# Zero matmuls in a fused attention and feed-forward kernel: only into PSUM banks without a planned reader, and a larger part of each planned PE gap

## The chip, the core and the metric

The kernel runs on one core of one Trainium2 chip. The metric is the device time of one execution in microseconds (us). A profile shows one execution, instruction by instruction; its "span" is the time from the first to the last instruction, in us from its own start. Engines: PE does matmuls (and PEld its weight loads), DVE, ACT and POOL do elementwise work, SP issues transfers. PSUM is the memory that PE writes into.

## What is computed

Inputs: q, k and v (8 batches, 12 heads, 448 positions, 64 dimensions), two gains of 64, `w_in` (768 x 2048) and `w_out` (2048 x 768), all float32.

```python
q_n, k_n = rmsnorm(q, g_q), rmsnorm(k, g_k)          # over the 64 dimensions
scores = 1/8 * q_n @ k_n.T                           # per batch and head
attn = exp(scores - max); attn = attn / (sum(attn) + 1e-9)
x = (attn @ v), heads side by side                   # 3584 x 768
h = x @ w_in
out = (h * clip(h + 3, 0, 6) / 6) @ w_out            # 3584 x 768
```

## The kernel before

**The work.** The unit of attention is a pair of heads: 48 pairs P, six to a batch. For a pair, SP loads k, q (L509, L537, L503) and v (L516, L503). Squares `sq` (L558, L560), row sums `ssq` (L577, DVE) and the root `rs` (L583, L584, ACT) give the scale, and `qks` (L593, L600, L609) is the scaled q or k. For the first twelve pairs PE turns it by 64 x 64 transposes (L653) into a tile M, from which copies make `kq`, `kp` and `kb` (L522, L524, L525); later pairs are turned by a transfer. PE makes scores in S from `kp` or `kb` (L801, L806); ACT takes their exponential, `e` or `er` (L834); PE multiplies it with v and a column of ones, `va` or `var`, into X (L772, L890); DVE divides by the row sum (`rd` L908, `xn` L909, `xr` L913). `xn` is turned, for the first two batches by PE (L930), into `xT`. Then the feed-forward part: `w_in` against `xT` into M (L969), ACT's `t` (L975) and DVE's `gT` (L977), then `w_out` against `gT` (L994) and the copy `y`, which is stored.

**PSUM.** There are two score tiles S0 and S1 (of two banks each), one tile X of two banks, and two tiles M. The real results leave columns free: X's second bank holds results in its first 260 columns, S's first bank in its first 448. A wait is set by tile: any write into X waits for the earlier readers of X, whatever the columns.

**The order.** A planner lists every step with an estimate of its duration, goes over the list forward and backward, and fixes a start and an end for each step on each engine (`Plan.order`). The kernel is then written out in the order of the planned starts, so each engine's queue is in that order. By the plan the last step ends at 433.06 us. At run time only semaphores count, not the planned times.

**The zero matmuls.** `zero` is a tile of zeros. Where the plan leaves PE idle for more than 0.3 us before a planned start of 115 us (`FILL_TO`), `fill` (L1105 on) writes matmuls of `zero` with `zero` (L1112) into the free columns of X (240 wide), S0 or S1 (64 wide); they add zero to what stands there and change no result. `reads` holds, for each of the three places, the planned start and end of every step on another engine than PE that uses its tile. `fill` walks through the gap in planned time: it takes the first place of X, S0, S1 that it may use at that moment, and moves on by an estimate of what the matmul takes; if there is none, it moves on by 0.1 us:

```python
if not any(x - 0.05 < t0 < y + 0.2 for x, y in l):
    n = t.shape[-1]
    nc.tensor.matmul(out=t, lhsT=zero[:, 0:128], rhs=zero[:, 0:n], start=False, stop=False,
                     skip_group_check=True)
    t0 += n / 1200 if t0 < COLD else n / 2400 / FILL
```

So a place is refused only while one of its readers is running by the plan. A zero matmul written just after a reader's planned end waits for that reader by semaphore, and the next real matmul of PE's queue stands behind it.

Of the kernel before, what the change touches and what calls it, by code (L numbers as in the profile page):

```python
# [304 lines left out]
def kernel(  # L305
# [80 lines left out]
    plan = Plan(NUDGES, ENGINES, HOLD)  # L386
    add = plan.add

    FILL, FILL_FROM, FILL_TO, COLD = 0.7, 1.2, 115.0, 6.0
    XPE, TQ, MOVE = 2, 0.26, 12  # L390
    GATE, W_IN_AT, W_OUT_AT, W_STEP = 4, 6.0, 40.0, 4.3
    START, FIRST, PAIR = 9.0, 3.7, 2.1
# [709 lines left out]
    reads = [(t, [(s.start, s.end) for used in ring.log[k::ring.n] for s in used if s.eng != "PE"])  # L1102
             for ring, k, t in idle]

    def fill(t0, t1):  # L1105


        while t1 - t0 > 0.1:
            for t, l in reads:
                if not any(x - 0.05 < t0 < y + 0.2 for x, y in l):  # L1110
                    n = t.shape[-1]
                    nc.tensor.matmul(out=t, lhsT=zero[:, 0:128], rhs=zero[:, 0:n], start=False, stop=False,  # L1112
                                     skip_group_check=True)
                    t0 += n / 1200 if t0 < COLD else n / 2400 / FILL
                    break
            else:
                t0 += 0.1

    with tc.manual_schedule():
        nc.vector.memset(zero[:], 0.0)  # L1120
        for t in (X_r.bufs[0][:], S_r.bufs[0][:], S_r.bufs[1][:]):
            nc.vector.memset(t, 0.0)
        holder, free = None, FILL_FROM
        for s in order:
            if s.eng == "PE":
                if s.start < FILL_TO and s.start - free > 0.3:
                    fill(free, s.start - 0.1)
                free = s.end
            ins = s.fn(s.eng)
            if ins is not None and s.lock and s.eng in ("DVE", "POOL"):  # L1130
                if s.eng == "POOL" and holder is not None:
                    tc.add_manual_dep(ins.ins, holder.ins.name, mybir.DependencyInfo(
                        mybir.DependencyClass.Sync, mybir.DependencyReason.DATA), reason="port")
                holder = ins if s.eng == "DVE" else None
# [30 lines left out]
```

## Time and profile before

| | |
|---|---|
| median of five runs | 435.73 us (433.9 to 439.19) |
| profiled execution: its time, its span | 435.73 us, 433.8 us |
| mean granted PE clock | 0.996 |
| busy: PE, DVE, ACT, POOL | 96%, 56%, 58%, 48% |
| zero matmuls (L1112) | 98 into X, 50 into S |
| first matmul of the feed-forward part (L969) | at 48.36 us |
| last matmul ends | at 429.2 us |

The views used: the page's shares; the busy time by stretch, whose columns are the stretch and its length, busy us and instructions of PE, PEld, DVE, ACT and POOL, the granted PE clock (PEclk, 1.00 is full speed), the mean busy share of the core's 16 DMA engines (it passes 1 where packets overlap) and GB/s; the chain of waits, that is the work that ended last, followed back from step to step (start, length, engine, tile and line); the view of one line, with what PE stood idle for before it (total us, times); and the timeline (start, length, engine, line, operation, number of instructions, and in brackets an idle time ahead and what ended it). An entry of several matmuls is as long as from the first start to the last end, and their ends are modelled, so it overlaps its neighbour by up to 0.2 us.

### The profile page before, as it was taken

What the parts mean: (1) busy time and instruction counts of PE and PEld (TensorE: products, weight loads), DVE (VectorE), ACT (ScalarE), POOL (GpSimd) and SP (SyncE); (2) the same over time, 40 slices, a digit from 0 to 9 for tenths busy, and PEclk for the clock granted to TensorE, in tenths of its full rate; (3) what the DMA queues carried; (4) which work ended last, traced back from release to release, by engine and by line L of the source; (5) the groups of instructions that cost most, each with busy time, mean ns of one, the idle gap of its engine ahead of it and who ended that gap; (6) DMA issues with size and microseconds to landing.
All of it is one profiled execution on the core that took longest, in us unless ns stands there. A gap on an engine that the chain in (4) does not pass through costs nothing.

```text
span 433.8 us, 10149 instructions
## 1 busy us (share of the span) xinstructions
PE 416.3 (96%) x4057; PEld 244.1 (56%) x4057; DVE 241.4 (56%) x472; ACT 249.8 (58%) x454; POOL 210.1 (48%) x270
## 2 busy tenths in 40 slices
PE   7867999999999999999999999999999999999995
PEld 5545665655456665655556566655555565644563
DVE  6757786655685565637753676445754545344300
ACT  5948877657874776517663676427763656023211
POOL 5845576475957254757554663665856210000000
PEclk9989999999999999999999999999999999999999
DMA  8999999669777946796667787485474330310122
GB/s 223 230 233 271 245 237 204 165 138 222 180 182 127 206 111 154 170 221 149 139 154 210 139 151 184 109 213 141 100 172 106 77 73 19 82 52 0 38 73 73
DMA packets 114838, 64.75 MB, mean 149 GB/s; under 512 B 71272, under 2 KB 111336, under 8 KB 114792
## 3 DMA queue, kind: packets, MB, share of 16 engines
q1 hardware_dynamic: 107488, 57.83, 56.8%
q0 software_dynamic: 7296, 6.29, 9.0%
q8 instruction: 31, 0.51, 0.5%
q14 instruction: 15, 0.12, 0.1%
q10 hardware_dynamic: 8, 0.00, 0.0%
HBM read 45.61 MB, written 11.01 MB: 131 GB/s over the span
## 4 chain that ended last, share of the span: by engine, by line
PE 87%; DMA 5%; DVE 4%; SPq 1%; ACT 1%; issue 1%; POOL 0%; DVEq 0%; ACTq 0%; POOLq 0%
PE M L969 28%; PE M L994 28%; PE X L890 9%; PE S L801 7%; PE S L994 4%; PE S L969 2%; DMA vf<-in_v_dram 2%; PE X L994 2%; PE S L806 2%; PE X L772 1%; DMA kf<-in_k_dram 1%; PE X L969 1%; DMA qf<-in_q_dram 1%; PE M L653 1%; DVE ssq L577 1%; DVE xn L909 1%
## 5 line engine op out<-in xcount | busy, mean ns | idle before, releaser
L969 PE MATMUL M<-xT,w_in_sb 128*128 128x384 bf16 (+1 forms) x696 | 142.7, 350 | 0.2
L834 ACT ACTIVATE e<-S 128x896 bf16<-128x896 f32 x144 | 124.8, 914 | 30.3 <-PE S L801 30.0
L994 PE MATMUL M<-w_out_sb,gT 128*128 128x384 bf16 x736 | 129.5, 326 | 0.0
L994 PEld LDWEIGHTS <-gT 128*128 128x128 bf16 x896 | 84.7, 98 | 54.5 <-issue 0.7
L969 PEld LDWEIGHTS <-w_in_sb 128*128 128x128 bf16 x768 | 71.8, 98 | 63.9 <-issue 2.1
L975 ACT ACTIVATE t<-M 128x384 f32<-128x384 f32 (+1 forms) x116 | 62.5, 539 | 71.0 <-PE M L969 70.1
L977 DVE SCALAR_TENSOR_TENSOR gT<-t,M 128x384 bf16<-128x384 f32 (+1 forms) x116 | 71.0, 613 | 57.5 <-ACT t L975 56.0
L577 DVE TENSOR_REDUCE ssq<-sq 128x14 f32<-128x896 f32 (+1 forms) x49 | 51.7, 1061 | 5.9 <-POOL sq L560 4.5
L890 PE MATMUL X<-va,e 128*128 128x65 bf16 x1152 | 50.8, 194 | 3.9 <-POOL va L524 3.5
L890 PEld LDWEIGHTS <-e 128*128 128x128 bf16 x1152 | 44.7, 98 | 16.9 <-issue 8.3
L560 POOL TENSOR_TENSOR sq<-qf 112x512 f32<-112x512 f32 (+1 forms) x38 | 39.2, 1034 | 22.5 <-DVE kp L675 8.2
L524 DVE COPY y<-M 128x384 f32<-128x384 f32 x40 | 22.3, 558 | 42.6 <-PE M L994 41.8
L600 POOL TENSOR_TENSOR qks<-kf,rs 128x384 bf16<-128x384 f32 x36 | 29.8, 828 | 29.4 <-ACT rs L584 24.5
L560 POOL TENSOR_TENSOR sq<-kf 128x384 f32<-128x384 f32 (+1 forms) x40 | 33.4, 837 | 19.4 <-DVE kp L675 8.1
L801 PE MATMUL S<-kq,kp 64*128 64x448 bf16 x288 | 41.3, 357 | 0.5 <-ACT kq L522 0.3
L609 POOL TENSOR_TENSOR qks<-qf,rs 112x512 bf16<-112x512 f32 x36 | 37.6, 1045 | 7.3 <-ACT rs L584 5.6
L524 POOL CAST va<-vf 128x384 bf16<-128x384 f32 x46 | 23.1, 506 | 32.2 <-PE X L890 15.3
L909 DVE TENSOR_TENSOR xn<-X,rd 128x384 bf16<-128x384 f32 x48 | 26.8, 558 | 1.7
L834 ACT ACTIVATE er<-S 128x896 bf16<-128x896 f32 (+1 forms) x27 | 22.5, 833 | 8.3 <-PE S L806 8.2
L583 ACT ACTIVATE rs<-ssq 128x14 f32<-128x14 f32 (+1 forms) x49 | 10.5, 214 | 25.6 <-DVE ssq L577 25.3
L908 DVE RECIPROCAL rd<-X 128x8 f32<-128x8 f32 x48 | 9.9, 205 | 21.8 <-PE X L890 20.9
L1112 PE MATMUL X<-zero 128*128 128x240 bf16 x98 | 16.0, 302 | 5.9 <-DVE xn L909 2.5
(79 smaller groups left out, 302.1 us busy)
## 6 DMA issues: line engine op xcount, KB each, us to landing
qf<-in_q_dram SPq DMA_DIRECT2D x48, 224.0 KB, 3.8
kf<-in_k_dram SPq DMA_DIRECT2D x36, 192.0 KB, 3.5
vf<-in_v_dram SPq DMA_DIRECT2D x36, 192.0 KB, 3.3
out_dram<-y SPq DMA_DIRECT2D x18, 192.0 KB, 3.0
w_in_sb<-in_moe_w_in_dram POOLq DMA_DIRECT2D x4, 768.0 KB, 14.2
w_out_sb<-in_moe_w_out_dram POOLq DMA_DIRECT2D x4, 768.0 KB, 19.6
kf<-in_k_dram SPq DMA_DIRECT2D x12, 224.0 KB, 5.3
vf<-in_v_dram SPq DMA_DIRECT2D x24, 96.0 KB, 9.0
```

The source lines that it names most:

```text
L524: return (nc.vector if e == "DVE" else nc.gpsimd).tensor_copy(out=out, in_=x)
L560: return engines[e].tensor_tensor(out=o, in0=x, in1=x, op=MULT)
L577: lambda i0=i0, i1=i1, rows=rows: nc.vector.tensor_reduce(out=ssq[0:rows, i0:i1], in_=sq[0:rows, i0:i1], axis=AX_X, op=ADD),
L609: return engines[e].tensor_tensor(out=qks[0:PT, NS:QB].rearrange("p t (h d) -> p h t d", h=2), in0=qf[0:PT].rearrange("p (h t) d -> p h t ...
L801: fns.append(lambda ps=ps, a=a, t=t, kp=kp, rhs=rhs: nc.tensor.matmul(out=ps[:, a, 0:S], lhsT=kp[a * 64:a * 64 + 64, t * 128:(t + 1) * 128 ...
L834: lambda dst=dst, ps=ps, w=2 if whole else 1: nc.scalar.activation(out=dst, in_=ps[:, 0:w, 0:S], func=EXP), s, *(AVW[P] if t < NS else AVR ...
L890: nc.tensor.matmul(out=X[:, a, s * E1:(s + 1) * E1], lhsT=e[:, t, a, c0:c0 + 128], rhs=va[:, a * NS + t, :], start=False, stop=(t == NS - ...
L909: nc.vector.tensor_tensor(out=xn[:], in0=xv[:, 0:NS, :, 0:D], in1=rd[:, 0:NS].unsqueeze(3).to_broadcast([128, NS, 2, D]), op=MULT)
L969: nc.tensor.matmul(out=m[:, 0:n], lhsT=w_in_sb[:, kt, f * 128:(f + 1) * 128], rhs=X[:, kt, :], start=(kt == 0), stop=(kt == NKT - 1))
L975: r = add("ACT", 0.17 + n / 1200, due + span, lambda: nc.scalar.activation(out=t[:, 0:n], in_=m[:, 0:n], func=RELU, bias=0.5, scale=1.0 / ...
L977: g = add("DVE", 0.155 + n / 960, due + span, lambda: nc.vector.scalar_tensor_tensor(out=G[:, f, :], in0=t[:, 0:n], scalar=1.0, in1=m[:, 0 ...
L994: nc.tensor.matmul(out=m[:, 0:HALF], lhsT=G[:, f, i * 128:(i + 1) * 128], rhs=w_out_sb[:, f, cols], start=(f == 0), stop=(f == NFT - 1))
```

## The change

It touches `fill`, the call of it and two constants. A place may now be used only if each of its planned readers either starts after the next real PE step (`now`) or has ended at least 0.4 us before the moment in question. The share of a gap that is charged to a zero matmul (`FILL`) goes from 0.7 to 0.9, so more of them go into a gap; the moment until which PE's clock is taken as half (`COLD`) goes from 6.0 to 7.0 us; and gaps from 0.2 us on are filled.

```diff
-    FILL, FILL_FROM, FILL_TO, COLD = 0.7, 1.2, 115.0, 6.0
+    FILL, FILL_FROM, FILL_TO, COLD = 0.9, 1.2, 115.0, 7.0
...
-    def fill(t0, t1):
+    def fill(t0, t1, now):
...
-                if not any(x - 0.05 < t0 < y + 0.2 for x, y in l):
+                if all(x > now or y + 0.4 < t0 for x, y in l):
...
-                if s.start < FILL_TO and s.start - free > 0.3:
-                    fill(free, s.start - 0.1)
+                if s.start < FILL_TO and s.start - free > 0.2:
+                    fill(free, s.start - 0.1, s.start)
```

The plan itself does not change: the queues of DVE, ACT, POOL and SP hold the same instructions in the same order, and PE's real matmuls keep theirs. The zero matmuls of the built kernels differ in these gaps (by the step that follows the gap, with its start in the profile before):

| next real PE step | zero matmuls before | after |
|---|---|---|
| the gaps before 22 us, in all | 74 X | 82 X |
| L801 at 22.93 | 11 S1 | none |
| L772 at 31.15 | none | 1 S1 |
| L801 at 34.05 | 7 S1 | none |
| L801 at 39.37 | 5 X, 6 S1 | none |
| L653 at 43.87 | 2 X, 2 S1, 2 S0 | none |
| L930 at 47.59 | 2 X, 18 S1 | 33 S1 |
| L806 at 47.98 | 1 X, 4 S0 | 10 S0 |
| L969 at 50.74 | 4 X | 5 X |
| L969 at 59.22 | 2 X | 3 X |
| L806 at 64.45 | 3 X | 14 S1 |
| L969 at 55.15, L653 at 70.86 | none | 1 X each |
| L969 at 67.13 | none | 4 S0 |
| L801 at 73.98 | none | 3 S0 |

## The prediction

> **What bounds the kernel now.** I first read the page's busy shares (PE 96%, DVE, ACT and POOL 48 to 58%), then the busy time by stretch.
>
> ```profile
> 23.90:27.50 3.60, 0.09 (x6) 0.10 (x1) 0.69 (x2) 2.23 (x4) 0.95 (x2) 1.00 1.18 247
> 27.50:31.00 3.50, 3.49 (x59) 2.45 (x58) 1.63 (x5) 1.73 (x4) 2.83 (x5) 0.56 1.19 234
> 37.00:48.00 11.00, 7.69 (x184) 6.20 (x183) 8.24 (x19) 8.77 (x19) 6.53 (x9) 1.00 1.19 260
> 100.00:433.80 333.80, 328.74 (x2856) 186.54 (x2853) 175.09 (x331) 178.34 (x312) 145.39 (x173) 1.00 0.56 129
> ```
>
> The first number after the length is PE's busy time; PEclk comes before the DMA share. From 100 us on PE is idle only in the tail after the last matmul (429 us): whatever brings the dense stretch forward brings the end forward. The holes are before 48 us. The chain of waits says what stands in them:
>
> ```profile
> 17.35 9.03 DMA vf<-in_v_dram
> 27.51 1.20 PE X L890 x24
> ...
> 37.98 0.57 DVE xn L909
> 38.59 0.67 PE X L1112 x5
> ...
> 46.87 0.36 PE X L1112 x2
> 47.23 0.53 PE S L1112 x18
> 47.76 0.17 PE M L930 x3
> ```
>
> Until 27.5 us a load of V sets the pace. Behind it the zero matmuls (L1112) themselves stand on the chain, after the DVE operation that read their bank. The view of L1112 says how long PE stood before them:
>
> ```profile
>   DVE xn L909: 2.5, 2
>   DVE X L1122: 2.2, 1
>   DVE xr L913: 1.3, 2
> ...
>   ACT er L834: 0.7, 2
> ```
>
> 2.2 is the start; the rest, 4.5 us, falls in six places of the timeline: A 22.52 (0.29), B 33.75 (0.43), C 38.59 (1.58), D 43.46 (0.84), E 46.87 (0.89), F 64.15 (0.43). Two of them in full:
>
> ```profile
> 36.66 0.35 PE L806 MATMUL S<-kq,kb 128*128 128x448 bf16 x1
> 38.59 0.67 PE L1112 MATMUL X<-zero 128*128 128x240 bf16 x5 [1.58 <-DVE xn L909]
> 39.37 0.36 PE L801 MATMUL S<-kq,kp 64*128 64x448 bf16 x2
> 39.67 0.34 PE L930 MATMUL M<-ident,xn 128*128 128x128 bf16 x3
> ...
> 46.87 0.36 PE L1112 MATMUL X<-zero 128*128 128x240 bf16 x2 [0.89 <-DVE xn L909]
> 47.07 0.69 PE L1112 MATMUL S<-zero 128*128 128x64 bf16 x18
> 47.59 0.33 PE L930 MATMUL M<-ident,xn 128*128 128x128 bf16 x3
> ```
>
> **The change, part by part.** The instruction lists differ on PE only, in zero matmuls: 148 become 162 (98 into X and 50 into S become 97 and 65). Spacing of one: seven X in 0.89 us with a last of 0.266, (0.89-0.27)/6 = 0.10 us; 18 S in 0.69 with a last of 0.19, 0.50/17 = 0.029 us. Each place is costed by asking when the next real matmul could have started.
>
> Before 27.5 us: ten X are added from 8 us on (0.1 to 0.2 us a gap, some of it in waits of 0.2 to 0.6), two before fall away, and A loses its 11 S and its wait. All of it lies ahead of PE's idle 24.0 to 27.5, which a transfer ends: 0. Without that cover it would be about +0.8 for the X and -0.6 for A.
>
> B (no zeros left): L801 (34.05) needs only the S bank that `e` (32.35 + 0.92) frees, so 33.35. The transposes L653 behind it (34.34) need the M tile that DVE's kq copy (33.75 + 0.38) reads: 34.2. PE gains 0.13; the exponentials behind, about 0.4 on ACT. Taken: 0.1, but 0 in the sum, because C waits for DVE.
>
> C (no zeros left): L801 can start when `e` (36.71 + 0.92) frees S, 37.6; L930 when xn ends, 37.98 + 0.56 = 38.54, so 38.6 in place of 39.67. Also xr (39.30) waited 0.76 for the zeros in X, and L772 (40.14) for xr: xr would end near 38.85, L772 start near 38.95. Gain 1.07 by L930, 1.19 by L772: -1.1. Queued behind are L890, L653, DVE's rd and kq, ACT's `e`: all wait for PE here (ACT 1.23 us, DVE 1.08 us), so they move along. Bounds: 0 if they don't, -1.6 if DVE too moves by B's 0.4.
>
> D (no zeros left): L653 (43.87) needs its M tile, which DVE's xT (43.44 + 0.36 = 43.80) reads: 0.05. Taken: 0.
>
> E (2 X and 18 S become 33 S): these S wait for no reader. They start where L890 ends (45.97) and take 33 x 0.029 = 0.96 us, to 46.93; L930 follows at about 46.95, not 47.59. Then 10 S in place of 1 X and 4 S: 0.29 against 0.22. What the dense stretch waits for is ACT's xT (47.96 + 0.49, then L969 at 48.5); ACT is free from kq at 47.50. So 0.46 of the 0.64 counts: -0.5.
>
> [...] The trace's loads do last 98 ns, but they overlap: the 18 S came 29 ns apart. [...] I take the row, which is this very instruction.
>
> F (3 X become 14 S): L969 has issued by about 63.6; 14 x 0.029 = 0.4, to 64.0. L806 needs kb, which DVE ends at 63.38 + 0.51 = 63.89: 64.05 in place of 64.45: -0.4 (0 to -0.5).
>
> Added where PE has hardly an idle moment: one X each in four gaps between 50 and 71 us, 4 x 0.10, and three S before L801 at 73.98, 0.1: +0.5. Four S (0.1) come before L969 at 67.13, which waits for gT (66.53 + 0.56): 0; uncovered, +0.1. One S before L772 at 31.15 is left out (0.03).
>
> Sum: C -1.1, E -0.5, F -0.4, added +0.5 = -1.5 us. The profiled execution took 435.73 with a span of 433.8, so 1.9 around it; 432.3 + 1.9 = 434.2. Its time equals the median of the runs, which lie between 433.9 and 439.19: the gain is smaller than their spread.
>
> **The clock.** PEclk is 0.56 in 27.5 to 31.0, after PE's idle of 3.5 us. Row: L890 x24 takes 1.20 us there against 0.94 later, L653 x14 0.58 against 0.41, L801 x2 0.56 against 0.36; over the seven groups between 27.5 and 31.5, 1.2 us. [...] By the row the closed window is in both kernels, and costs nothing new. [...]
>
> **The rivals.**
> *The gain is taken up by other work before 66 us.* For: DMA share is about 1.2 until 66 us, and two POOL waits (47.59 and 49.45) are put down to loads of q. Against: PE waits for no DMA after 27.5, and what POOL makes there (qks) is next taken by PE in L653 at 58.45. If true, half or more is lost: -0.7 to 0, 435.4.
>
> *The clock closes more often:* -1.5 + 1.2 = -0.3, 435.4. [...]
>
> *The change doesn't do what it says.* The fill goes by planned times, and from 38 us on the execution is some 6 us behind the plan; if ACT and PE drift apart, the chosen S bank has a reader after all and new waits replace the old. Against: in 46 to 64 us all engines lag alike, and E's S bank is read next at 49.98. About 435.7.
>
> *Slower: the zeros in S bring their whole weight load.* At the 98 ns of the rows, E's 33 and 10 and F's 14 cost 57 x (0.098-0.029) = 3.9 us more: -1.5 + 3.9 = +2.4, 438.1. It decides from 1.5/57 + 0.029 = 0.055 us for one on; the rows have 0.029.
>
> **How the numbers follow.** Forecast 0.52; taken up 0.20; clock closed more often 0.08, less often 0.07; doesn't do it 0.07; slower 0.06. The forecast's own range is 433.7 (C at -1.6) to 435.0 (C and F at half). The whole range is 432.6 to 436.1: it reaches to the lucky clock below, to no gain plus the runs' noise above, and leaves out the slower case. One per cent is 4.4 us, about what a measurement of this kernel can tell from no change. No case reaches that alone: faster by over 1% 0.03 (all gains and a lucky clock), slower 0.03 (whole weight loads and a closed window), within 0.94.
>
> **What would show it.** Right: no wait before L1112 on xn, xr or er after 10 us; L801 after L806 near 37.6 with L930 1 us behind it; L930 before L969 about 1.7 us earlier, and L969's first at about 46.8; PE's idle ahead of L890 at 27.5 as before or longer. Wrong: zeros in S more than 0.05 us apart; new waits of L1112 on `e`; L969 early but L653 near 58 to 62 us at its old time; PEclk below 0.9 in another stretch.

## The result, and the profile after

| | before | after |
|---|---|---|
| median of all runs | 436.43 us (47 runs, 433.76 to 440.39) | 434.1 us (26 runs, 432.87 to 435.35) |
| profiled execution: its time, its span | 435.73, 433.8 us | 433.18, 431.4 us |
| mean granted PE clock | 0.996 | 0.992 |

The ratio of after to before is 0.9944 (95%: 0.9929 to 0.996), that is 2.4 us less (1.7 to 3.1; 436.43 x 0.0056, and the same with the ends). The forecast was 1.5 us less, at 434.2 us.

The busy time by stretch of the kernel after (columns: stretch, length, busy us and instructions of PE, PEld, DVE, ACT and POOL, PEclk, DMA share, GB/s):

```profile
23.90:27.50 3.60, 1.31 (x26) 1.33 (x24) 0.69 (x2) 1.30 (x3) 1.34 (x3) 0.71 1.18 249
27.50:31.00 3.50, 3.50 (x57) 2.28 (x55) 2.60 (x8) 1.95 (x4) 2.93 (x5) 0.50 1.20 223
37.00:48.00 11.00, 9.04 (x198) 6.91 (x197) 9.11 (x21) 10.21 (x22) 6.68 (x9) 1.00 1.19 261
100.00:431.40 331.40, 326.24 (x2828) 185.12 (x2824) 173.91 (x330) 176.44 (x309) 143.24 (x170) 1.00 0.57 128
```

PE is busy 9.04 of the 11 us between 37 and 48, where it was 7.69; part of this is more zero matmuls, and the stretch now reaches some 2 us further into the work. From 100 us on it is as dense as it was (98%). The half clock of 27.5 to 31 us is still there, and now complete: 0.50.

The view of L1112 of the kernel after, with what PE stood idle for before it (us, times):

```profile
its engine sat idle before it (us, times) until:
  DVE X L1122: 2.2, 1
  issue: 2.0, 4
  DVE zero L1120: 1.0, 1
```

Every wait on xn, xr and er is gone; 2.2 and 1.0 belong to the start. The chain of waits of the kernel after (start, length, what), in the same places as before:

```profile
17.13 7.95 DMA vf<-in_v_dram
...
26.22 1.48 PE X L890 x24
...
34.40 0.29 PE M L930 x3
34.71 0.36 DVE xT L524
35.07 0.54 DVE sq L560
35.66 0.45 issue
36.12 1.09 DVE ssq L577
37.20 0.13 DVE rd L908
37.35 0.57 DVE xn L909
37.92 0.04 issue
37.96 0.34 PE M L930 x3
...
44.24 0.96 PE S L1112 x33
45.21 0.27 PE M L930 x3
```

V still sets the pace until 26.2 us. At 38 us L930 now follows xn directly, with no zero matmul between. The same two places in the timeline of the kernel after:

```profile
36.02 0.35 PE L806 MATMUL S<-kq,kb 128*128 128x448 bf16 x1
36.87 0.36 PE L801 MATMUL S<-kq,kp 64*128 64x448 bf16 x2 [0.50 <-ACT e L834]
37.96 0.34 PE L930 MATMUL M<-ident,xn 128*128 128x128 bf16 x3 [0.73 <-DVE xn L909]
...
44.08 1.12 PE L1112 MATMUL S<-zero 128*128 128x64 bf16 x33
45.14 0.34 PE L930 MATMUL M<-ident,xn 128*128 128x128 bf16 x3
```

L801 now stands ahead of the wait for xn (it starts 0.85 us after L806, where it was 2.71), and L930 comes 1.94 us after L806, where it was 3.01. The 33 zero matmuls start without a wait and take 44.24 to 45.21 in the chain.

To see where the 2.4 us of span come from I measured the time between the starts of the same real PE groups, read from the timelines (us):

| stretch | before | after | difference |
|---|---|---|---|
| start to L890 (ended by the load of v) | 27.51 | 26.22 | -1.29 |
| L890 to L653 (half clock) | 5.40 | 6.41 | +1.01 |
| L653 to L806 (place B) | 3.75 | 3.39 | -0.36 |
| L806 to L653 (C, D) | 7.21 | 6.12 | -1.09 |
| L653 to L969 (E) | 4.49 | 3.86 | -0.63 |
| L969 to L969, 14 us (three added X) | 14.21 | 14.29 | +0.08 |
| L969 to L969 (F) | 2.26 | 1.77 | -0.49 |
| L969 to L801, 12 us (1 X, 4 S, 3 S added) | 11.55 | 11.74 | +0.19 |
| L801 to the end | 357.44 | 357.59 | +0.15 |

The last L801 starts at 76.38 us before and at 73.80 after; the three S stand ahead of it, and not of the L801 at 73.98 as the table of the gaps above has it. The first two rows nearly cancel: where the load of v ends its wait, L890 starts at 25.99 us with the denser fill alone and at 27.61 with the first bridge, and the second row goes with how long PE's clock stays half (3.4 us before, 6.8 after; last section). Whether the change has a part in either is not shown. The other rows sum to -2.15. These are what the change does.

### The profile page after: what moved, and what is told of

The parts are those of the page before. It is cut to its first block, busy times and chain, and to the rows that moved or that the text cites. A ratio compares the mean times of both kernels' runs of the same rounds, so it can differ in the third digit from the quotient of the medians.

```text
span 431.4 us, 10177 instructions
## 1 busy us (share of the span) xinstructions
PE 416.2 (96%) x4071; PEld 244.9 (57%) x4071; DVE 241.1 (56%) x472; ACT 249.8 (58%) x454; POOL 210.3 (49%) x270
## 4 chain that ended last, share of the span: by engine, by line
PE 88%; DMA 5%; DVE 3%; ACT 1%; issue 0%; POOL 0%; DVEq 0%; POOLq 0%; ACTq 0%
PE M L969 28%; PE M L994 28%; PE X L890 9%; PE S L801 7%; PE S L994 4%; PE S L969 2%; DMA vf<-in_v_dram 2%; PE X L994 2%; PE S L806 2%; PE M L653 1%; DMA qf<-in_q_dram 1%; PE X L772 1%; DMA kq<-qks 1%; PE X L969 1%; DVE ssq L577 1%; DMA grow<-in_g_k_dram 1%
## 5 line engine op out<-in xcount | busy, mean ns | idle before, releaser
L969 PE MATMUL M<-xT,w_in_sb 128*128 128x384 bf16 (+1 forms) x696 | 142.7, 350 | 0.2
L969 PEld LDWEIGHTS <-w_in_sb 128*128 128x128 bf16 x768 | 71.9, 98 | 63.9 <-issue 2.2
L890 PEld LDWEIGHTS <-e 128*128 128x128 bf16 x1152 | 45.4, 99 | 15.8 <-issue 7.3
L890 PE MATMUL X<-va,e 128*128 128x65 bf16 x1152 | 51.5, 196 | 2.6 <-POOL va L524 2.3
L801 PE MATMUL S<-kq,kp 64*128 64x448 bf16 x288 | 41.5, 359 | 0.8 <-ACT e L834 0.7
L801 PEld LDWEIGHTS <-kp 64*128 64x128 bf16 x288 | 9.1, 94 | 20.8 <-issue 17.9
```

The source lines that it names most:

```text
L801: fns.append(lambda ps=ps, a=a, t=t, kp=kp, rhs=rhs: nc.tensor.matmul(out=ps[:, a, 0:S], lhsT=kp[a * 64:a * 64 + 64, t * 128:(t + 1) * 128 ...
L890: nc.tensor.matmul(out=X[:, a, s * E1:(s + 1) * E1], lhsT=e[:, t, a, c0:c0 + 128], rhs=va[:, a * NS + t, :], start=False, stop=(t == NS - ...
L969: nc.tensor.matmul(out=m[:, 0:n], lhsT=w_in_sb[:, kt, f * 128:(f + 1) * 128], rhs=X[:, kt, :], start=(kt == 0), stop=(kt == NKT - 1))
```

## The experiments

Theory W (waiting): the old zero matmuls waited for readers of their bank and so delayed real work; the gain is that delay. Its rival K (clock): what counts is the denser fill, which holds PE's clock. A third, N: the zero matmuls bring nothing at all by this point of the kernel. None of the kernels leaves out part of the computation, since zero matmuls add nothing to the result. All ratios are to the kernel before, with 95% intervals.

**Each half of the change alone.** The rule for the banks without the denser fill (129 zero matmuls), and the denser fill with the old rule (180):

```diff
# rule_only, against before
-    def fill(t0, t1):
+    def fill(t0, t1, now):
-                if not any(x - 0.05 < t0 < y + 0.2 for x, y in l):
+                if all(x > now or y + 0.4 < t0 for x, y in l):
-                    fill(free, s.start - 0.1)
+                    fill(free, s.start - 0.1, s.start)
# dense_only, against after
-                if all(x > now or y + 0.4 < t0 for x, y in l):
+                if not any(x - 0.05 < t0 < y + 0.2 for x, y in l):
```

> The kernel before with the new rule on banks alone; the shares, the cold time and the smallest gap are as before (129 zero matmuls in place of 148). Theory W (the gain is that zero matmuls no longer wait for the readers of their bank): C -1.1, E -0.6, F -0.4 as in the changed kernel, without the +0.5 of added zeros: -2 us or a little more, at least as fast as the changed kernel (ratio near 0.995 or below). Theory K (the gain is the denser fill, which keeps the clock up): no gain, ratio 1.000, or slower, since four gaps are left empty.

> The changed kernel with the old rule on banks: larger share, longer cold time, gaps from 0.2 us on (180 zero matmuls). Theory W: the waits on xn, xr and er before zero matmuls stay, and some 30 zeros more stand ahead of real work: +0.3 to +1 us, ratio 1.001 to 1.003. Theory K: this part holds the gain, ratio near 0.995.

Measured: the rule alone 0.9929 (0.9903 to 0.9955), 434.1 us; the denser fill alone 1.0003 (0.9981 to 1.0026), 437.87 us. The rule is the whole gain. The clock does not explain it: where the granted clock of an execution is 0.990 or less, the kernel before takes 437.53 us (median of 24) and the kernel after, on the same chip, 434.87 (median of 12). The view of L1112 of the kernel with the denser fill alone still has the old waits:

```profile
  DVE xn L909: 1.4, 2
  DVE xr L913: 1.3, 2
  DVE zero L1120: 1.0, 1
  DVE xT L524: 0.5, 1
  ACT er L834: 0.3, 1
```

**One place alone: C.** Before, without the 11 zero matmuls ahead of L801 at 39.37:

```diff
-                if s.start < FILL_TO and s.start - free > 0.3:
+                if s.start < FILL_TO and s.start - free > 0.3 and s.n != 228:
```

> The kernel before without the zero matmuls of one gap, the one before L801 at 39.37 us (5 into X, 6 into S). Theory W: -1.1 us (ratio 0.9975), with L930 about 1.1 us earlier against the L653 that precedes the gap. Theory K: 0, or slower if the gap was needed for the clock.

Measured: 0.9958 (0.9938 to 0.9978), or -1.8 us (-1.0 to -2.7). The timeline of this kernel:

```profile
37.76 0.35 PE L806 MATMUL S<-kq,kb 128*128 128x448 bf16 x1
38.67 0.36 PE L801 MATMUL S<-kq,kp 64*128 64x448 bf16 x2 [0.56 <-ACT e L834]
39.70 0.34 PE L930 MATMUL M<-ident,xn 128*128 128x128 bf16 x3 [0.67 <-DVE xn L909]
```

L806 to L930 takes 1.94 us in place of 3.01, -1.07, as after the whole change; the stretch L806 to L653 is 6.15, and all later stretches are those of before (4.49, 14.21, 2.26, 11.55, 357.44). So 11 zero matmuls, which took PE 0.78 us (38.59 to 39.37 in the timeline of before), held up all that follows by 1.07 us. The trace gives this number; the ratio has the same sign and is too coarse to size it.

**One place alone: B.** Before, without the seven zero matmuls ahead of L801 at 34.05 (`s.n != 192` in the same line):

> The kernel before without the zero matmuls of one gap, B (7 into S, before L801 at 34.05 us). My sum took this as 0, since C waits for DVE; the segment of the changed kernel's trace from L653 to L806 around it was 0.36 us shorter. If that is B's: ratio 0.999, and 0.3 to 0.5 us less from L653 to L806 than in the kernel before at the same clock. If it is 0: 1.000 and the same segment.

Measured: 0.9987 (0.9967 to 1.0007). L653 to L806 takes 3.39 us in place of 3.75, the later stretches are those of before (7.21, 4.49, 14.21, 2.26, 11.55, 357.46). The ratio does not tell -0.36 us from nothing. This stretch also varies between kernels without any zeros at B: it takes 3.39 us after, 3.56 with the rule alone, 3.72 with zeros until 27 us (these two are at half clock until 35.5 and 36.1 us) and 3.83 with the last bridge below. So compare kernels that stay at half clock equally long, for 10.2 us, three times the 3.41 us that I call a window (last section): the one without C's zeros, which keeps B's, takes 10.73 us from L890 to L806, those with the rule alone and with zeros until 27 us, which have none at B, 10.22 and 10.43. B is worth 0.3 to 0.5 us in the trace.

**The price of a zero matmul in S.** After, with 66 in place of 33 at E:

```diff
+                if s.n == 264:
+                    for _ in range(33):
+                        nc.tensor.matmul(out=idle[2][2], lhsT=zero[:, 0:128], rhs=zero[:, 0:64], start=False,
+                                         stop=False, skip_group_check=True)
```

> The changed kernel with 66 zeros in place of 33 at E, ahead of L930. By the spacing of the trace, 0.029 us: +0.96 us against the changed kernel, all of it on the path; ratio to before 0.9966, the 66 in 1.9 to 2.1 us. By a whole weight load each, 0.1 us: +3.3 us, ratio 1.002, the 66 in 6.5 us.

Measured: 0.9959 (0.9942 to 0.9977). The timeline of this kernel, with the added ones as L1130:

```profile
45.27 1.12 PE L1112 MATMUL S<-zero 128*128 128x64 bf16 x33
46.23 1.13 PE L1130 MATMUL S<-zero 128*128 128x64 bf16 x33
47.19 0.33 PE L930 MATMUL M<-ident,xn 128*128 128x128 bf16 x3
```

From start to start, 33 take 0.96 us: 29 ns each. E's stretch grows from 3.86 to 4.71, +0.85, and the stretches from there to L801 are as long as in the kernel after (14.30, 1.77, 11.74), so nearly all of it is passed on. The ratio lies above the kernel after's (0.9944, and 0.9949 again), with intervals that overlap. At 98 ns each, the length of a weight load in the rows, it would have been +3.2.

**Fewer and none.** After with zero matmuls only before 27 us of the plan (83 of them), and with none at all (`FILL_TO` 0), and the kernel after once more beside a second copy of the latter:

```diff
-    FILL, FILL_FROM, FILL_TO, COLD = 0.9, 1.2, 115.0, 7.0
+    FILL, FILL_FROM, FILL_TO, COLD = 0.9, 1.2, 27.0, 7.0     # to_27
+    FILL, FILL_FROM, FILL_TO, COLD = 0.9, 1.2, 0.0, 7.0      # no_fill
```

> The changed kernel without any zero matmul behind the planned time of 27 us (83 are left), so without the 33 and 10 at E and the 14 at F. Theory W: the real matmuls at E and F wait for xn and kb anyhow, and the X added between 48 and 100 us fall away: 0.5 to 1 us faster than the changed kernel (ratio to before 0.992 to 0.994). Theory K: PE's clock closes in another window after 27 us: 1 to 2 us slower than the changed kernel, with PEclk below 0.9 in a stretch beyond 35 us.

> The changed kernel without any zero matmul. Theory W: the waits at B, C, E and F are gone here too, but PE is thinly busy from 2 to 24 us, so the clock stays at half for most of the first 36 us: +1 to +5 us against the changed kernel, ratio to before 0.997 to 1.006. Theory N (a zero matmul only costs PE time, and the clock is no matter): as fast as the best kernel so far, 0.992 or below.

> The changed kernel again, as the partner of the others on one chip, and a second sight of its clock after 27 us: ratio to before 0.993 to 0.996; PEclk at half for one, two or three windows of 3.4 us, by chance.

> No zero matmul at all, again. If zero matmuls bring nothing in this kernel (theory N): 1 to 2 us faster than the changed kernel beside it, ratio to before near 0.991. If the first result was luck of the clock: as the changed kernel or slower, ratio 0.994 or above.

Measured: until 27 us 0.9934 (0.9914 to 0.9955), 433.72 us; none 0.9912 (0.9885 to 0.994), 432.58 us, and again 0.9912 (0.9881 to 0.9944), 433.22 us; the kernel after again 0.9949 (0.9931 to 0.9967), 434.74 us. The kernel without any zero matmul is at least as fast as the changed one (the intervals overlap a little): N holds, K falls, and I had expected the opposite of "none", that a cold start would cost. The cold start is there. The timeline of the kernel without zeros:

```profile
20.39 0.58 PE L653 MATMUL M<-ident,qks 64*64 64x64 bf16 x14
...
22.41 0.41 PE L653 MATMUL M<-ident,qks 64*64 64x64 bf16 x14
```

Until 22 us L653 x14 takes 0.58 us, as it does at half clock (0.58 in the kernel before at 29.13 us, PEclk 0.50; 0.41 at 32.91, PEclk 1.00). With zeros the clock opens earlier: the zeros in X start 0.20 us apart until 7.4 us in the kernel before and until 4.9 us in the kernel after, and 0.10 to 0.12 us apart behind. But the chain of waits of this kernel shows why it costs nothing:

```profile
17.36 7.86 DMA vf<-in_v_dram
...
25.36 0.94 POOL va L524 x2
26.30 0.04 issue
26.35 1.48 PE X L890 x24
```

V's load ends at the same time, and L890 starts at 26.35 us (after: 26.22). Everything that PE does earlier is hidden behind that load at either clock: PE waits 2.1 us for `va` here, 2.29 after. From there on the stretches are those of the kernel after or less: 1.57 for F (after 1.77), 11.55 for the next (after 11.74). These 0.4 us are what the zero matmuls of the kernel after still cost in the trace. The times of the same chip put it at 1.5 us (433.22 against 434.74), from seven and 17 runs; the rest is not explained.

**A bridge.** If zero matmuls can hold the clock at all, it is in the idle time before L890, which all kernels above leave mostly empty. The rule alone with 22 X there; the same with zeros only before 27 us; no other zeros and 30 X there:

```diff
                 free = s.end
+                if s.n == 169:
+                    for _ in range(22):
+                        nc.tensor.matmul(out=idle[0][2], lhsT=zero[:, 0:128], rhs=zero[:, 0:240], start=False,
+                                         stop=False, skip_group_check=True)
```

> The kernel with the new bank rule alone, plus 22 zero matmuls into X (2.2 us) ahead of the L890 that waits for a load of v near 24 to 27 us. PE stands idle there for 2.1 to 3.6 us and PEclk is 0.5 for one to three windows of 3.4 us afterwards. If that clock costs what its groups show (about 1 us a window): 1 to 3 us faster than with the new rule alone (ratio to before 0.986 to 0.991) and PEclk 1.00 from 25 to 36 us. If the transfers set the pace up to 36 us anyway: no gain, ratio 0.993, and L890 at 27 us and L801 at 38 us as before.

> As the one with 22 zeros before L890, and no other zero matmul behind the planned time of 27 us. Theory W: real work after 27 us gains what the fill there costs, 0.1 to 0.5 us against that kernel (ratio 0.985 to 0.990). Theory K: the clock closes near 37 to 48 us, where PE idles for 0.5 to 1.2 us several times: slower than that kernel by 1 us or more.

> No zero matmul but 30 into X (3 us) ahead of the L890 that waits for v. If a closed window after 27 us costs 0.7 us and the 30 keep the clock up through the wait: up to 2 us faster than without any, ratio 0.987 to 0.990. If the gate closes all the same, as it did behind 22 zeros: no gain, ratio 0.991 or, where v comes early and the zeros are in its way, 0.993.

Measured: 0.9918 (0.9884 to 0.9951), 0.9924 (0.9898 to 0.9951) and 0.9906 (0.9879 to 0.9934). In the profiles of the second and third the clock is full from L890 on; in the first it closes all the same, from 29.42 to 36.25 (PEclk 0.68, 0.50 and 0.97 from 28 us on, by 4 us). Busy time by stretch, first of the bridge with the rule alone, then of the bridge with no other zeros:

```profile
28.00:32.00 4.00, 3.74 (x74) 2.73 (x70) 2.96 (x9) 2.04 (x4) 3.31 (x5) 0.68 1.20 213
32.00:36.00 4.00, 4.00 (x54) 2.23 (x54) 2.53 (x6) 3.09 (x6) 1.89 (x3) 0.50 1.15 276
```

```profile
24.00:28.00 4.00, 4.00 (x41) 3.28 (x40) 1.49 (x4) 2.23 (x4) 1.13 (x3) 1.00 1.18 249
28.00:32.00 4.00, 3.74 (x86) 2.87 (x84) 2.42 (x8) 2.04 (x4) 3.29 (x5) 1.00 1.21 220
```

Where the clock stays full, L890 to L806 takes 8.25 and 8.26 us (the latter from 28.32 to 36.58); in the kernel without zeros, with two closed windows, 9.80, as in the kernel after (26.22 to 36.02). So a bridge has 1.5 us to win in the trace, but the times do not show it: 0.9906 against 0.9912 for none. For the 30 zeros the timeline shows one reason:

```profile
25.14 3.34 PE L1131 MATMUL X<-zero 128*128 128x240 bf16 x30
28.32 0.93 PE L890 MATMUL X<-va,e 128*128 128x65 bf16 x24
```

L890 follows the zeros without a wait for v. POOL's `va` ended at 27.38 us (26.43 + 0.95), and in the kernels before, after and without zeros L890 starts 0.05 to 0.06 us behind it; so here the bridge itself held L890 up by about 0.9 us. The 22 zeros of the second bridge end in time, but do not hold the clock in every execution: in seven of 16 the granted clock is 0.998 or more and the median 431.1 us, in the other nine it is 0.988 to 0.997 and the median 434.6. An early load of v could bring both the fuller clock and the shorter time, so what the clock alone is worth there stays open.

## Why the prediction was right, and where its terms were off

*C, forecast -1.1: -1.07* by L930, in the kernel after and in the kernel with C alone. What is queued behind moved along, as taken: the stretches after it did not grow.

*B, forecast 0.1 and counted as 0: -0.3 to -0.5.* This is the mis-sized term. I set it to nothing "because C waits for DVE", and took DVE as fixed. But DVE's chain to that xn begins at PE's L930: in the chain of the kernel after, L930 at 34.40 releases xT, behind which sq, ssq, rd and xn stand on DVE (with 0.45 us between sq and ssq, about as before). When B lets L930 go earlier, xn comes earlier by as much. I had this as the bound of C ("if DVE too moves by B's 0.4"); the bound was the value.

*E, forecast -0.5: -0.63.* I let 0.46 of the 0.64 count, since ACT would be free of its kq copy only at 47.50. That copy did stay (it starts 3.10 us after D's L653 before, 3.09 after), but the xT copy comes 0.58 us sooner: after the change it starts 0.42 us after kq's start (45.65 and 45.23), although kq is listed with 0.53. My 0.46 left out this overlap of the rows. *F, forecast -0.4: -0.49*, at its bound.

*Added zeros, forecast +0.5: +0.27* (0.08 and 0.19; 0.42 at most with the last row, which varies by 0.8 between profiles). Part of them fell into short waits for other work. *A and D: 0, as taken.* A's wait is gone and V's load covers it: without any zeros L890 starts no earlier than the load lets it.

With these sizes the sum is -0.4 - 1.1 - 0.6 - 0.5 + 0.3 = -2.3 us, beside the measured -2.4 (-3.1 to -1.7); the forecast's -1.5 is outside this interval. The absolute 434.2 came closer to 434.1 than the terms deserve: the median of before over all runs is 436.43 and not 435.73. Of the signs, L969's first came at 46.00, where I had 46.8, and PE's idle ahead of L890 was shorter and not as long (2.29 us, 3.52 before): v's load happened to end earlier in this profile.

*The zeros in S, 29 ns apart.* The zeros' weight loads last 98 ns (median of L1112 on PEld, before and after); that a zero matmul in S takes only the 29 ns of their spacing was read from one group of 18. The slower rival's +2.4 counts all 57 at 98 ns. In the kernel after the 33 take 0.96 us, 29 ns each, and doubling them added 0.96 us from start to start. So the slower rival falls. *The rival "taken up by other work"* falls too: from L969 at 62 us to the end the time is 369.33 us after (11.74 + 357.59) and 368.99 before (11.55 + 357.44). *"Doesn't do what it says"* falls with the view of L1112, in which PE has no new wait. ACT has one: its `e` stood 0.8 us for the one zero matmul in S ahead of L772. From L890 to L653 it took 6.41 us with that and 6.40 without any zeros, at two closed windows each, so it cost nothing there. *The clock:* the half clock lasts 3.42 us before (27.94 to 31.36) and 6.82 after (25.42 to 32.24), so one window of 3.41 us and two. The price I gave one window, 1.2 us, was too high for the trace, where it is 0.7 to 0.8: L890 to L806, with no zeros at B, takes 8.25 us with none, 9.80 with two (after) and 10.22 and 10.43 with three (rule alone, zeros until 27 us). The rival "closes more often" did happen in the profiled pair, and the earlier load hid it. The lower end of the range, 432.6, took 1.2 us off for a clock that closes less often: no run shows what would bring that about, and over the runs the granted clock was 0.986 to 0.994 after.

Still open: what sets the number of closed windows (last section), and why the runs of the kernel before spread over 6.6 us and those after over 2.5. A part of the first spread goes with the clock: on the three chips of the experiments the kernel before takes 435.4 to 435.5 us (medians; 25 executions) where its granted clock over the span is 0.995 or more, and 437.1 to 437.6 (95) where it is 0.990 or less. No execution of the kernel after reached 0.995.

## What to carry to other kernels

That its engine is idle does not make filler work free: it takes part in the dependencies of the tile that it writes, and real work queued behind it inherits its waits (at C the zeros stood 1.58 us behind xn, and L930 came 1.07 us later than without them), so place it only where no reader is due, and ask first whether leaving it out is as fast. When a wait goes away, do not take the other engines as fixed: follow the chain of the operation that ends last back to where it begins, since that may be the very instruction that moves. A start-up penalty that ends before a long load ends costs nothing, and work to avoid it gains nothing: here the half clock until 22 us left L890 at 26.35 us, against 26.22.

## What the runs showed of the hardware

*The half clock's length is not set by PE being busy.* From 24 to 40 us, read from PEclk by 4 us, the clock was half for 3.4 us in the kernel before, for 6.8 after, without zeros, with E doubled and with the first bridge, and for 10.2 with the rule alone, the denser fill alone, C alone and zeros until 27 us: one, two or three windows of 3.41 us. In the kernel with the rule alone (busy time by stretch; closed from 25.28 to 35.52) PE is busy without a break and the clock stays half:

```profile
28.00:32.00 4.00, 4.00 (x66) 2.73 (x64) 2.55 (x8) 2.04 (x4) 3.39 (x5) 0.50 1.20 215
32.00:36.00 4.00, 4.00 (x57) 2.38 (x54) 3.00 (x7) 2.74 (x6) 1.95 (x3) 0.56 1.17 274
```

The window of 3.41 us from 28.69 to 32.11 lies in this: PE is busy for all of it, and the clock stays half. In the kernel before PE is as busy from 27.94 to 31.35, with the same 1.67 us of transposes (L653, L930) in it, and the clock opens behind it.

Nor was PE wholly idle ahead of the closing. In the first kernel with a bridge the clock went to half at 29.42 us, after this:

```profile
26.00:29.42 3.42, 1.91 (x43) 1.31 (x42) 0.81 (x3) 0.54 (x1) 2.39 (x4) 1.00 1.18 243
```

PE was busy for 1.91 of its 3.42 us. In the kernel after the clock went to half at 25.42 us, with 1.65 us busy in the 3.41 before; in the kernel before at 27.94, with 0.43. PE's busy time alone does not decide it either: in the second bridge PE was busy for 1.67 of the 3.40 us from 24 to 27.4, less than the first bridge's 1.91, and PEclk is 1.00 in every stretch up to 48 us. What else counts, no run tells.

*The clock column can show full clock where the work runs at half.* In the kernel without zeros the busy time by stretch shows full clock in

```profile
4.00:8.00 4.00, 1.21 (x29) 1.07 (x29) 2.94 (x8) 2.67 (x9) 0.97 (x2) 1.00 1.00 292
```

while L653 x14 takes 0.58 us until 22 us, the length it has at half clock, against 0.41 after. The kernel before shows 1.00 from 4 to 7.4 us too, with its zeros in X 0.20 us apart. So in this early part the length of a known instruction tells the clock, and not the column.
